# Four early chunks read in one step, two chunks by scan, q and k in two transfers, and a new order of the whole program

## The chip, the cores and the metric

The kernel runs on one core of one Trainium2 chip. The metric is the device time of one execution in microseconds (us). An execution under the profiler gives a trace; other executions give times alone.

## What is computed

Three things in a row: a gated recurrence over time (mLSTM) for 4 batches and 8 heads of 768 steps with head size 40, and then two pairs of dense layers on its output, which is laid out as 3072 tokens of 320 values.

```python
for t in range(S):
    m_new = np.maximum(f_gate[:, :, t] + m, i_gate[:, :, t])
    f_stab = np.exp(f_gate[:, :, t] + m - m_new)
    i_stab = np.exp(i_gate[:, :, t] - m_new)
    C = f_stab * C + i_stab * outer(vt, kt)
    n = f_stab * n + i_stab * kt
    y[:, :, t] = sigmoid(o_gate) * (C @ qt) / np.maximum(np.abs(n @ qt), 1.0)
x = y as (3072, 320)
h = x @ w_in                       # 320 -> 2048
g = np.where(h >= 1, h, np.where(h <= -1, 0.0, (h + 1) ** 2 / 4))
x = g @ w_out                      # 2048 -> 320
h = x @ w2_in
r = np.maximum(h, 0.0)
out = (r * r) @ w2_out
```

## The kernel before

**The recurrence by chunks.** Time is cut into six chunks of 128 steps per batch, 24 chunks in all, ordered chunk 0 of the four batches, then chunk 1 of the four, and so on. Each chunk is two halves of 64 steps. `attention(n, ...)` plans the steps of one chunk. TensorE makes the scores of queries and keys and the products of keys and values for the state (`scores`), VectorE weighs the scores by decay factors (`weigh0`, `weigh1`) and updates the state (`Ca`, `Cb`), and TensorE then reads: the part inside a half (`intra`: weighed scores times values) plus the part from the state (`inter`: query times state).

**Two ways to read.** For the first four chunks (`WIDE = 4`) the read is two steps. `cross` makes the products that go from one half of the partitions to the other, `after` copies a small piece out of them (tile `tiny`), and `read` waits for that copy and makes the rest (`read` and `cross` are recorded on line 904). For the other twenty chunks the read is one step, `wide`: near products (line 904) into the output tile and far products (line 962) into the free part of the score tiles, taken in turn so that all four 64x64 quarters of TensorE's array have work. What landed in the score tiles is then moved (`move1`, `move0`, into tile `yx`) and added (`join1`, `join0`, line 977) by ScalarE and VectorE.

**Two ways to make the decay factors.** For chunks 0 and 1 (`c <= SUMC`), eight chunks in all, they come from `rise` (a product of a mask and the log factors, line 739), `sums` (TensorE, lines 745, 748 and 752: running sums of logs) and an exponential on ScalarE. For the others the raw factors are loaded from a DRAM copy (`ld_f`, tensor `f_all`) and run through a scan on VectorE (`decay`, line 774); the values are then scaled by the input gate first (`v_in`, line 799).

**The dense layers.** The first pair of layers runs in 8 blocks of 3 chunks, the second in 6 blocks of 4 chunks; each block goes over 16 slices of the hidden size. Per block and slice there are 8 products into tile `h` (line 1131), an activation on ScalarE, VectorE and GpSimd, and 3 products per chunk into tiles `acc0`, `acc1`, `acc2` and `v` (line 1191). Numbers are split into a high and a low part, so each product is made more than once. The weights are stored as 64-bit floats and are taken apart on chip when they first come (lines 499 to 551).

**What sets the order.** Nothing runs in the order in which it is written. Each step is put into a `Plan` with its engine, a rank, a duration as the author takes it, and what it needs. `Plan.order()` walks through time with these durations and takes, on each engine, the ready step of the lowest rank; where a step may go to several engines it takes the one that would end first. The result is one fixed order per engine. The ranks come from tables of numbers (`MOVE`, `SHIFT_OF`, `FINE`), the choice of engine also from `PICK`. `LAT["SP"]` is the time from the end of a transfer's issue to its data. Where the plan has nothing for TensorE, it puts one of `FILL = 140` idle steps, two small products each (line 1274), so 280 in all, that keep TensorE active.

**Start.** SyncE (SP) issues all transfers from one queue. The gates come in two parts (lines 574 and 582). A chain of scans and products on VectorE, GpSimd and ScalarE makes logs and factors from them, which TensorE transposes (lines 620 and 661); only then can the first `rise` and `sums` run.

**From one part to the next.** From the tenth chunk on, the output of a chunk goes to DRAM by four transfers (`scatter`, line 433) and comes back transposed by three (`gather`, lines 436 and 438), all issued by SP, before its block can start. The output of a first dense block goes the same way to the second part.

Of the kernel before, what the change touches and what calls it, by code (L numbers as in the profile page):

```python
# [39 lines left out]
class Plan:  # L40
# [7 lines left out]
    LAT = {"T": 0.25, "SP": 1.9}  # L48
# [134 lines left out]
def pool(n):  # L183
# [28 lines left out]
}  # L212
SHIFT_OF = {
    "g": {"v1": 110.65, "v1f": -135.75, "v1i": -162.53, "masks": 80.77, "ft": -115.13, "fc": 118.96,
        "a3": -39.22, "tp": -127.3, "cp": -87.45, "a2": -58.39, "p1": 4.03, "a1": -74.68, "p2": -6.2,
        "v2": -223.95, "d1": -233.43, "d2": 196.83},
    "w": {"load": 53.07, "a_move": 94.67, "v_clamp": -3.04, "a_tail": 53.39, "v_top": -13.26,
        "v_join": 70.33, "a_hi": 176.02, "v_lo": 73.74, "lo": 162.56, "sub": -82.64, "put": 44.29,
        "clamp": 68.16, "top": -29.18},
    "x": {"ld_qk": 35.32, "ld_vko": 9.45, "rise": -96.86, "sums": -140.56, "grow": -39.2, "sumsa": -33.31,  # L220
        "growa": 2.76, "k_in": 53.09, "sig": 9.42, "sigma": -42.83, "q_in": 16.55, "scores": -12.57,
        "update": -52.52, "scale": 48.33, "weigh0": -85.03, "weigh1": 19.6, "cross": -50.09, "after": 5.03,
        "read": -20.72, "norm_a": -53.03, "norm_b": 97.64, "norm_c": 36.58, "tr": 3.8, "hi": 22.16,
        "lo": -67.91, "ld_f": 46.74, "ld_a": -16.53, "decay": 84.93, "v_in": -41.91, "wide": -47.73,
        "move1": -71.31, "join1": -42.21, "move0": 16.41, "join0": -65.28, "turn": 80.21, "store": -67.91,
        "load": -12.79, "again": -79.17, "rise1": -46.24, "sums1": 3.17},
    "y": {"load": 227.79, "hi": 109.08, "lo": 229.83},
    "d": {"mm1": 8.22, "relu": 72.6, "square": 34.95, "gate": -54.05, "hi": 16.25, "lo": 54.66, "mm2": 11.36,
        "keep": -54.24, "evac": -38.36, "turn": -51.89, "store": 169.37},
}  # L230
FINE = {
    "g0": {"v1": -57.95, "v1f": -31.12, "v1i": 73.83, "masks": 45.91, "ft": 91.47, "fc": 26.6, "a3": -16.28,
        "tp": -50.47, "cp": -121.18},
    "g1": {"v1": 97.2, "v1f": 61.71, "v1i": -10.95, "a2": -29.43, "p1": 77.88, "a3": -55.68, "a1": -102.99,
        "p2": -199.57, "v2": 37.26, "d1": -99.65, "d2": -161.28, "tp": 115.56, "cp": 250.13, "ft": -12.8,
        "fc": 74.2},
    "w0": {"load": -48.87, "a_move": -182.32, "v_clamp": 70.39, "a_tail": -9.72, "v_top": 22.93,
        "v_join": -60.58, "a_hi": -60.75, "v_lo": -70.85, "lo": 33.59, "clamp": 7.25, "top": 98.67},
    "w1": {"load": -23.77, "a_move": -21.6, "v_clamp": -53.77, "a_tail": -209.41, "v_top": -57.83,
        "v_join": -140.2, "a_hi": -147.14, "v_lo": -50.52, "lo": -201.67, "clamp": 96.23, "top": -86.1},  # L240
    "w2": {"load": 10.02, "a_move": -103.33, "v_clamp": -20.23, "a_tail": 103.18, "v_top": 18.06,
        "v_join": -156.63, "a_hi": 35.17, "sub": -158.96, "put": -66.82, "clamp": 10.62, "top": 12.98},
    "w3": {"load": 42.08, "a_move": 28.86, "v_clamp": 48.51, "a_tail": 42.67, "v_top": -19.28,
        "v_join": -49.33, "a_hi": 192.52, "sub": 27.7, "put": 13.53, "clamp": 14.13, "top": 39.95},
    "w4": {"load": 20.87, "a_move": 23.82, "v_clamp": 40.5, "a_tail": -13.26, "v_top": 33.13,
        "v_join": 119.88, "a_hi": 70.78, "sub": 81.87, "put": -64.08, "clamp": -55.62, "top": -54.18},
    "w5": {"load": -21.16, "a_move": -42.33, "v_clamp": -72.31, "a_tail": 133.19, "v_top": 74.43,
        "v_join": 126.61, "a_hi": 139.07, "sub": -41.56, "put": -106.72, "clamp": 4.0, "top": 58.13},
    "w6": {"load": 35.35, "a_move": 10.88, "v_clamp": -43.5, "a_tail": 100.1, "v_top": -34.69,
        "v_join": -1.42, "a_hi": 104.74, "sub": -20.29, "put": -136.89, "clamp": -79.27, "top": 6.17},  # L250
    "w7": {"load": 86.26, "a_move": 120.67, "v_clamp": -119.39, "a_tail": -66.48, "v_top": -68.52,
# [1148 lines left out]
```

## Time and profile before

| | |
|---|---|
| runs without profiler, 3 | median 827.92 us (827.0 to 828.84) |
| profiled execution | 832.61 us, span in the trace 830.9 us |
| mean granted TensorE clock | 0.994 of full |
| busy: TensorE products | 819.8 us, 99% |
| busy: VectorE (DVE) | 387.1 us, 47% |
| busy: ScalarE (ACT) | 459.0 us, 55% |
| busy: GpSimd (POOL) | 365.8 us, 44% |

The span is what lies between the first and the last recorded instruction; the profiled execution took 1.7 us more than its span, and 4.7 us more than the median of the runs without a profiler. A busy TensorE is not a TensorE at its peak: products are pipelined, so the recorded duration of one contains time in which others run; how long a step takes is read from the starts of what stands before and behind it.

### The profile page before, as it was taken

The page shows a single profiled execution, that of the slowest core. Times are in us where ns is not written, and L with a number is a line of the kernel's source. Part 1 is how long each engine was busy: PE and PEld are TensorE (multiplying, and loading weights), DVE is VectorE, ACT ScalarE, POOL GpSimd, SP SyncE. Part 2 cuts the span into 40 slices and gives each one's busy share as a digit, 9 for nine tenths or more (in the row PEclk, how much of TensorE's full clock was granted, in tenths as well). Part 3 has the DMA queues.
Part 4 walks back from the last instruction along what each step waited for, and adds up shares of the span by engine and source line. Part 5 has one row for each costly group of instructions (what it writes and reads, how often), then busy time and mean ns, then how long its engine had stood idle before and what let it go on. Part 6 is the DMA issues. An engine that isn't in the chain of part 4 may idle for free.

```text
span 830.9 us, 18844 instructions
## 1 busy us (share of the span) xinstructions
PE 819.8 (99%) x7536; PEld 753.4 (91%) x7536; DVE 387.1 (47%) x760; ACT 459.0 (55%) x897; POOL 365.8 (44%) x387
## 2 busy tenths in 40 slices
PE   8999999999899999999999999999999999999998
PEld 7668899999899999999999988999899898998997
DVE  5678879785676555544225655312121111111111
ACT  4667678866456556555678867443433433433432
POOL 3133220042353467682677566534533534433333
PEclk9899999999999999999999999999999999999999
DMA  8467564435443464521313541002110100100000
GB/s 229 162 220 237 166 172 151 141 108 124 109 116 92 110 150 125 160 56 31 70 41 99 164 98 67 1 0 70 29 42 1 45 26 1 52 1 0 32 1 33
DMA packets 93244, 73.41 MB, mean 88 GB/s; under 512 B 58944, under 2 KB 77372, under 8 KB 93156
## 3 DMA queue, kind: packets, MB, share of 16 engines
q1 hardware_dynamic: 93156, 72.21, 30.5%
q8 instruction: 59, 0.97, 0.5%
q14 instruction: 29, 0.24, 0.1%
HBM read 61.67 MB, written 10.51 MB: 87 GB/s over the span
## 4 chain that ended last, share of the span: by engine, by line
PE 91%; DMA 4%; SPq 1%; DVE 1%; ACT 1%; POOL 1%; issue 0%; POOLq 0%; DVEq 0%
PE h L1131 42%; PE acc L1191 34%; PE v L1191 5%; PE v L904 2%; PE s L850 2%; PE acc L1274 1%; PE s L857 1%; PE h L745 1%; DMA qk<-in_qk_dram 1%; DMA w<-in_gates_dram 1%; DMA vko<-in_vko_dram 1%; PE acc L550 1%; PE h L748 1%; SPq L433 1%; DMA x<-xn 1%
## 5 line engine op out<-in xcount | busy, mean ns | idle before, releaser
L1163 POOL TENSOR_TENSOR xTh<-xTl,xTh 128x512 fp32r<-128x512 f32 x96 | 124.1, 1292 | 177.1 <-ACT xTh L485 176.8
L1191 PE MATMUL acc<-w,g 128*128 128x320 f32 x1152 | 194.9, 312 | 0.1
L1151 DVE TENSOR_TENSOR xTl<-xTl,h 128x512 f32<-128x512 f32 x96 | 66.0, 688 | 245.3 <-ACT xTl L1138 245.3
L1191 PEld LDWEIGHTS acc<-w,g 128*128 128x128 f32 x1152 | 176.0, 188 | 3.3 <-ACT g L485 0.6
L1131 PE MATMUL h<-xTh,w 128*128 128x384 f32 x640 | 176.1, 340 | 2.4 <-ACT xTh L485 2.3
L1191 PE MATMUL acc<-w,xTh 128*128 128x320 f32 x864 | 142.5, 308 | 0.0
L1191 PEld LDWEIGHTS acc<-w,xTh 128*128 128x128 f32 x864 | 134.2, 188 | 8.2
L1131 PE MATMUL h<-qk,w 128*128 128x512 f32 x384 | 135.9, 395 | 0.0
L1131 PE MATMUL h<-xTl,w 128*128 128x384 f32 x384 | 129.9, 338 | 0.6 <-POOL xTl L1092 0.6
L1138 ACT ACTIVATE xTl<-h 128x512 f32<-128x512 f32 x96 | 57.4, 598 | 115.2 <-PE h L1131 112.1
L1131 PEld LDWEIGHTS h<-xTh,w 128*128 128x128 f32 x640 | 117.3, 188 | 3.8 <-ACT xTh L485 2.6
L1136 ACT ACTIVATE r<-h,half 128x384 f32<-128x384 f32 x128 | 74.0, 578 | 79.6 <-PE h L1131 68.2
L1149 DVE SCALAR_TENSOR_TENSOR r<-r,h 128x384 f32<-128x384 f32 x128 | 70.0, 547 | 78.8 <-ACT r L1142 73.5
L485 ACT ACTIVATE xTh<-xTl 128x512 fp32r<-128x512 f32 x96 | 60.7, 632 | 81.9 <-PE v L1191 80.1
L1131 PEld LDWEIGHTS h<-qk,w 128*128 128x128 f32 x384 | 72.1, 188 | 12.9
L1163 POOL TENSOR_TENSOR g<-r,g 128x384 fp32r<-128x384 f32 x63 | 66.3, 1053 | 36.0 <-ACT g L485 35.2
L485 ACT ACTIVATE g<-r 128x384 fp32r<-128x384 f32 x128 | 66.4, 520 | 21.2 <-PE acc L1191 18.3
L1131 PE MATMUL h<-vko,w 128*128 128x512 f32 x192 | 75.7, 394 | 0.0
L1131 PEld LDWEIGHTS h<-xTl,w 128*128 128x128 f32 x384 | 72.4, 188 | 0.9 <-POOL xTl L1092 0.9
L1142 ACT ACTIVATE r<-r 128x384 f32<-128x384 f32 x128 | 66.9, 523 | 2.9
L1131 PE MATMUL h<-d,w 128*128 128x512 f32 x192 | 60.3, 395 | 0.0
L1191 PE MATMUL v<-w,xTh 128*128 128x320 f32 x288 | 57.8, 309 | 0.0
(148 smaller groups left out, 1098.4 us busy)
## 6 DMA issues: line engine op xcount, KB each, us to landing
wraw<-in_wts_dram SPq DMA_DIRECT2D x32, 704.0 KB
vko<-in_vko_dram SPq DMA_DIRECT2D x24, 524.5 KB
d<-f_all SPq DMA_DIRECT2D x32, 128.0 KB
qk<-in_qk_dram SPq DMA_DIRECT2D x24, 160.0 KB
out_dram<-o SPq DMA_DIRECT2D x20, 160.0 KB
qk<-in_qk_dram SPq DMA_DIRECT2D x24, 128.0 KB
x<-x SPq DMA_DIRECT2D x24, 128.0 KB
ab<-a_all SPq DMA_DIRECT2D x20, 128.0 KB
```

The source lines that it names most:

```text
L433: nc.sync.dma_start(out=to[a], in_=t[32 * a:32 * a + 32].rearrange("r (b t) -> r b t", t=32))
L485: nc.scalar.activation(out=out, in_=in_, func=ACTF.Copy)
L850: nc.tensor.matmul(out=z["s"][a][u, U * h:U * h + U], lhsT=z["qk"][row[a], 0, h, u], rhs=z["qk"][row[a], 1, h, u], start=True, stop=True)
L904: nc.tensor.matmul(out=z["y"][sub[u], E * h:E * h + E], lhsT=lhsT, rhs=rhs, start=start, stop=True, skip_group_check=True)
L1131: nc.tensor.matmul(out=h, lhsT=a, rhs=b, start=(i == 0), stop=(i == 7))
L1136: nc.scalar.activation(out=r, in_=z["h"], func=ACTF.Relu, scale=0.5, bias=half)
L1138: nc.scalar.activation(out=r, in_=z["h"], func=ACTF.Relu)
L1142: nc.scalar.activation(out=z["r"], in_=z["r"], func=ACTF.Square)
L1149: nc.vector.scalar_tensor_tensor(out=r, in0=r, scalar=1.0, in1=z["h"], op0=ALU.min, op1=ALU.max)
L1151: nc.vector.tensor_mul(out=r, in0=r, in1=z["h"])
L1163: engine[e].tensor_sub(out=z["g1"], in0=z["r"], in1=z["g0"].bitcast(F32))
L1191: nc.tensor.matmul(out=acc[k][:, 0:DM], lhsT=a, rhs=b, start=(f == f0 and i == 0), stop=(f == f1 - 1 and i == 2))
```

## The change

- `WIDE` goes from 4 to 0: the first four chunks read by `wide` too. In chunk 0 the first half has no state yet, so its step has 24 products where a later chunk has 32; `move1` and `join1` follow, `move0` and `join0` do not.
- `SUMB = 2`: of the four chunks with `c == 1` only those of batches 0 and 1 make their factors by sums; batches 2 and 3 take `ld_f`, `decay` and `v_in`.
- `ld_qk` issues two transfers where it issued three: the first, of 64 rows, now brings k and q.
- The tile of `ft` is kept under a key of its own for each of the two gate parts.
- The planner's durations of transfers are other numbers, `LAT["SP"]` goes from 1.9 to 2.8, and all of `MOVE`, `SHIFT_OF`, `FINE` and `PICK` are new, so every engine's order is new.

```diff
-    LAT = {"T": 0.25, "SP": 1.9}
+    LAT = {"T": 0.25, "SP": 2.8}
...
 MOVE = {
-    "g": [-174.08, -251.94],
+    "g": [-393.49, -318.28],
...
-WIDE = 4
+WIDE = 0
 SUMC = 1
+SUMB = 2
...
-            t_["ft"] = t = new("s", [128, 512])
+            t_["ft", c0] = t = new("s", [128, 512])
...
-            plan.add(Y, rank + GDMA, 0.2, d1, [key["f0"] + e + (1,)], [("f0d", 0)])
+            plan.add(Y, rank + GDMA, 0.33, d1, [key["f0"] + e + (1,)], [("f0d", 0)])
...
+        summed = c < SUMC or c == SUMC and b < SUMB
...
-            for a, w, p in ((0, D, 0), (0, U, 1), (1, D, slice(0, 2))):
-                nc.sync.dma_start(out=z["qk"][U * a:U * a + w, p], in_=qk[n][0:w, p, 4 * a:4 * a + 4])
+            for a, w in ((0, U), (1, D)):
+                nc.sync.dma_start(out=z["qk"][U * a:U * a + w], in_=qk[n][0:w, :, 4 * a:4 * a + 4])
...
-        plan.add(Y, at - 11.5 , 2.1, ld_vko, make=[("vko", n)])
+        plan.add(Y, at - 11.5, 1.3, ld_vko, make=[("vko", n)])
         if c:
-            if c > SUMC:
+            if not summed:
...
-        fx = "h" if early or c == 1 else "s"
+        fx = "h" if early or c else "s"
...
-        if c <= SUMC:
+        if summed:
             plan.add({V: Shared(0.69), P: 1.35, A: 2.05}, at - 7.5 - SUMR * c, 0, rise, [("fmT", c), ("o", -1)], [("d1", n)])
...
-        if c > SUMC:
+        if not summed:
             plan.add(pb(H * E, H), at - 6, 0, v_in, [("vko", n), ("it", c)], [("vt", n)])
...
-            plan.add(Y, at + 0.4, 1.6, store, [("xn", n)], [("xnd", n)])
-            plan.add(Y, at + 0.5, 1.2, load, [("xnd", n)], [("x2", ("n", n))])
+            plan.add(Y, at + 0.4, 1.9, store, [("xn", n)], [("xnd", n)])
+            plan.add(Y, at + 0.5, 1.6, load, [("xnd", n)], [("x2", ("n", n))])
...
-    plan.add(Y, -40, 0.8, cst_rest, make=[("cst", 0)])
+    plan.add(Y, -40, 1.9, cst_rest, make=[("cst", 0)])
```

What the new tables move is seen in the order of the instructions. Three places follow; a row is a line of the program, the operation, and what it writes and reads (a number behind `x` counts equal rows), and "..." stands for rows left out.

**SyncE at the very start**, before:

```order
L709 DMA vko<-in_vko_dram 128x1049
L574 DMA w_178<-in_gates_dram 36x2x128
L576 DMA ident<-in_cst_dram 128x128
L499 DMA wraw<-in_wts_dram 128x1408
L582 DMA w_178<-in_gates_dram 36x2x640
L709 DMA vko<-in_vko_dram 128x1049
L499 DMA wraw<-in_wts_dram 128x1408
L705 DMA qk<-in_qk_dram 40x512
L705 DMA qk<-in_qk_dram 64x512
L705 DMA qk<-in_qk_dram 40x2x512
```

and with the change:

```order
L710 DMA qk<-in_qk_dram 64x2x512
L710 DMA qk<-in_qk_dram 40x2x512
L578 DMA w_173<-in_gates_dram 36x2x128
L580 DMA ident<-in_cst_dram 128x128
L503 DMA wraw<-in_wts_dram 128x1408
L710 DMA qk<-in_qk_dram 64x2x512
L710 DMA qk<-in_qk_dram 40x2x512
L586 DMA w_173<-in_gates_dram 36x2x640
L714 DMA vko<-in_vko_dram 128x1049
L503 DMA wraw<-in_wts_dram 128x1408
```

The second part of the gates (36x2x640) was the fifth transfer, behind one large `vko`; it is now the eighth, behind four transfers of q and k, and the first `vko` stands behind it.

**TensorE at the read of an early chunk**, before (tile `d_935` holds the weighed scores of the fourth chunk; lines 745 and 748 are the sums of another):

```order
L904 MATMUL v<-Ca,qt 64x41 x4
L1069 MATMUL s<-ident,xn 128x128 x3
L745 MATMUL h<-d_577,o 64x512 x2
...
L904 MATMUL v<-vko,d_935 64x41 x8
L904 MATMUL v<-Ca,qt 64x41 x4
L904 MATMUL v<-vko,d_935 64x41 x8
L550 MATMUL acc_165<-wt,ident 128x352
```

and with the change (the first chunk):

```order
L770 MATMUL h<-o,logs 64x64 x8
L909 MATMUL v<-vko,d_525 64x41 x2
L967 MATMUL s<-Ca,qt 64x41
L967 MATMUL s<-vko,d_525 64x41
...
L909 MATMUL v<-vko,d_525 64x41
L909 MATMUL v<-Ca,qt 64x41
```

The four products of `cross` stood apart, ahead of other work; now near and far products are one run, and the far ones go to tile `s`.

**SyncE at the store and reload of the twelfth chunk** (`xn_133`; `x_18`, `x_1` and `x_7` are outputs of the first dense part), before:

```order
L721 DMA ab<-a_all 40x512
L715 DMA d_3369<-f_all 64x512 x2
L433 DMA x_18_107<-pa 32x10x32 x4
L433 DMA x_1_90<-pa 32x10x32 x4
L433 DMA x_7_96<-pa 32x10x32 x4
L433 DMA xn_133<-xn 32x10x32 x4
L709 DMA vko<-in_vko_dram 128x1049
L436 DMA x_3567<-xn_133 128x2x128
L438 DMA x_3567<-xn_133 64x128 x2
```

and with the change:

```order
L437 DMA xn_133<-xn 32x10x32 x4
L714 DMA vko<-in_vko_dram 128x1049
L720 DMA d_3437<-f_all 64x512 x2
L714 DMA vko<-in_vko_dram 128x1049
L440 DMA x_3515<-xn_133 128x2x128
L442 DMA x_3515<-xn_133 64x128 x2
L437 DMA x_18_107<-pa 32x10x32 x4
L437 DMA x_1_90<-pa 32x10x32 x4
L437 DMA x_7_96<-pa 32x10x32 x4
```

The twelve transfers of the dense outputs stood ahead of the chunk's store; they now stand behind its reload.

Counted over the whole order: the idle products are 280 in both; 230 of them stood ahead of the first `sums`, now 246 do. Between the twelfth chunk's scores and the first product of the block that takes it in stood 6 groups of eight products of line 1131 and 78 products of line 1191; now there are 16 groups and 144 products. The runs of equal array form (64x64 quarters or the whole array) change 108 times before and 102 times with the change.

## Rows read from the trace of the kernel before

**Rows 1.** The page, part 1: busy time, share, instructions.

```profile
PE 819.8 (99%) x7536; PEld 753.4 (91%) x7536; DVE 387.1 (47%) x760; ACT 459.0 (55%) x897; POOL 365.8 (44%) x387
```

**Rows 2.** Waits of TensorE: who waited for whom, us in total, times, longest.

```profile
PE h L1131 <- ACT xTh L485: 2.3, 1, 2.3
PE s L620 <- POOL w L599: 1.9, 1, 1.9
...
PE v L904 <- DVE sg L1025: 0.7, 1, 0.7
```

**Rows 3.** Stretches: length; busy PE, PEld, DVE, ACT, POOL; granted clock, DMA share, GB/s.

```profile
20.00:25.00 5.00, 5.00 (x40) 5.00 (x39) 4.09 (x7) 2.86 (x4) 0.00 (x0) 0.50 0.67 214
...
50.00:150.00 100.00, 99.79 (x1288) 86.48 (x1287) 84.46 (x188) 75.64 (x159) 25.09 (x35) 1.00 0.55 174
...
200.00:250.00 50.00, 47.06 (x620) 44.57 (x619) 33.45 (x76) 25.75 (x55) 22.66 (x25) 0.97 0.43 109
```

**Rows 4.** Timeline of TensorE, 1 to 26 us: start, us, instruction.

```profile
1.26 12.78 PE L1274 MATMUL acc<-x 128*128 128x160 bf16 x160 [1.26 <-DVE w L578]
...
19.34 6.47 PE L1274 MATMUL acc<-x 128*128 128x160 bf16 x52
25.74 0.65 PE L745 MATMUL h<-d,o 64*64 64x512 f32 x2
```

**Rows 5.** Timeline of all engines, 0 to 45 us.

```profile
3.27 0.81 SPq L582 DMA_DIRECT2D w<-in_gates_dram  x1
...
5.22 2.10 SPq L705 DMA_DIRECT2D qk<-in_qk_dram  x3
...
10.34 1.54 DVE L592 TENSOR_TENSOR_SCAN w<-w,w 36x640 f32<-36x640 f32 x1 [0.69 <-DMA w<-in_gates_dram]
```

**Rows 6.** Timeline of TensorE, 40 to 110 us: reads, sums, a wide read.

```profile
43.17 0.25 PE L904 MATMUL acc<-Ca,qt 40*64 40x41 f32 x1
...
43.76 0.86 PE L550 MATMUL acc<-wt,ident 128*128 128x352 f32 x2
...
44.70 0.66 PE L904 MATMUL acc<-vko,d 64*64 64x41 f32 x16
...
45.90 0.27 PE L765 MATMUL h<-o,logs 64*64 64x64 f32 x1
...
60.53 1.08 PE L745 MATMUL h<-d,o 64*64 64x512 f32 x4
...
62.51 0.61 PE L904 MATMUL v<-vko,d 64*64 64x41 f32 x16
...
63.99 0.86 PE L550 MATMUL acc<-wt,ident 128*128 128x352 f32 x2
...
69.24 0.26 PE L904 MATMUL v<-vko,d 64*64 64x41 f32 x2
...
70.31 0.44 PE L1131 MATMUL h<-xTh,w 128*128 128x384 f32 x1
```

**Rows 7.** Timeline of SyncE's queue, 196 to 232 us.

```profile
211.27 5.86 SPq L433 DMA_DIRECT2D x<-pa  x12
```

**Rows 8.** The chain that ended last, 205 to 235 us: start, us, what.

```profile
206.13 1.52 PE acc L1191 x9
207.65 1.43 PE h L1131 x8
...
223.11 4.55 DMA x<-xn
...
229.42 2.32 PE h L1131 x7
```

**Rows 9.** Groups by line: busy us, mean ns of one, idle before.

```profile
L1274 PE MATMUL acc<-x 128*128 128x160 bf16 x280 | 25.8, 259 | 1.3 <-DVE w L578 1.3
```

**Rows 10.** Groups by line and form, VectorE: busy us, mean ns, idle before.

```profile
L774 DVE TENSOR_TENSOR_SCAN d<-d,eyes 128x512 f32<-128x512 f32 x16 | 20.2, 1264 | 13.1 <-PE s L962 13.0
...
L977 DVE TENSOR_TENSOR v<-s,yx 64x164 f32<-64x164 f32 x40 | 13.5, 338 | 2.0 <-ACT yx L485 0.7
```

More of the change, by code (lines that the diff above doesn't have):

```diff
@@ L220 @@
[L220 to L226, printed above, removed]
@@ L230 @@
+    "y": {"load": 181.09, "hi": 187.73, "lo": 276.44},
+    "d": {"mm1": 15.93, "relu": 96.16, "square": 31.54, "gate": -58.92, "hi": 128.93, "lo": 51.88,
+        "mm2": 18.41, "keep": -69.51, "evac": -57.39, "turn": -17.6, "store": 185.58},
 }
 FINE = {
[L232 to L236, printed above, removed]
@@ new lines @@
+    "w14": {"load": -57.58, "a_move": -39.21, "a_tail": 125.41, "v_top": -4.28, "clamp": 157.03,
+        "top": -4.65, "v_join": -38.99, "a_hi": 142.25, "v_lo": -36.37, "lo": -96.21},
+    "x0": {"ld_qk": -24.49, "ld_vko": 37.5, "rise": 22.48, "sums": -236.91, "grow": 23.29, "sumsa": -11.81,
+        "growa": -11.63, "k_in": 8.17, "sig": -143.29, "sigma": -82.1, "q_in": -162.17, "scores": -152.9,
+        "update": -97.61, "scale": -264.07, "weigh0": -168.27, "weigh1": 76.56, "cross": -21.08,
+        "after": -242.75, "read": -6.93, "norm_a": 37.85, "norm_b": -148.44, "norm_c": 63.94, "tr": 4.79,
+        "hi": 33.77, "lo": -247.23, "again": -25.03, "wide": -26.58, "move1": -98.78, "join1": -47.55},
@@ new lines @@
+    "x1": {"ld_qk": -49.09, "ld_vko": 8.73, "rise": -66.25, "sums": -21.24, "grow": -51.63, "sumsa": -3.58,
+        "growa": -54.77, "k_in": -145.19, "sig": -119.92, "sigma": -78.23, "q_in": -117.64, "scores": -187.4,
+        "update": 15.39, "scale": -33.91, "weigh0": -2.86, "weigh1": 352.02, "cross": -32.47, "after": 76.29,
+        "read": -38.74, "norm_a": -129.96, "norm_b": -60.93, "norm_c": -45.07, "tr": -62.29, "hi": -5.23,
+        "lo": -147.46, "again": 215.21, "wide": -101.25, "move1": -131.17, "join1": -156.55},
@@ new lines @@
+    "x2": {"ld_qk": -43.67, "ld_vko": -46.08, "rise": -0.12, "sums": 32.79, "grow": -95.11, "sumsa": 62.82,
+        "growa": -92.13, "k_in": -18.36, "sig": -148.62, "sigma": -190.57, "q_in": -182.77,
+        "scores": -152.84, "update": -15.28, "scale": -14.61, "weigh0": 122.39, "weigh1": 105.42,
+        "cross": -9.47, "after": 94.1, "read": -53.54, "norm_a": 3.86, "norm_b": -52.47, "norm_c": -61.37,
+        "tr": -25.92, "hi": -34.21, "lo": 110.55, "again": 57.68, "wide": -63.84, "move1": -135.82,
+        "join1": -208.24},
@@ new lines @@
+    "x3": {"ld_qk": 29.97, "ld_vko": -19.9, "rise": 53.45, "sums": 164.04, "grow": -49.09, "sumsa": 76.41,
+        "growa": -23.21, "k_in": 6.41, "sig": -53.99, "sigma": 139.4, "q_in": -25.85, "scores": -31.75,
+        "update": 32.8, "scale": -1.75, "weigh0": 208.34, "weigh1": 4.06, "cross": -129.77, "after": 128.44,
+        "read": -184.85, "norm_a": 6.35, "norm_b": -7.46, "norm_c": 6.3, "tr": 22.85, "hi": -51.43,
+        "lo": -147.34, "again": -202.46, "wide": -105.24, "move1": -71.28, "join1": -254.77},
@@ L1244, in dense @@
                 ok = ("pa", (part, n), 99)
-            plan.add(Y, g + 2, 0.7 if part else 1.6, store, [ok], [("st", (part, n))])
+            plan.add(Y, g + 2, 0.7 if part else 1.9, store, [ok], [("st", (part, n))])
     def x2_load(n, at):
```

237 lines of the change are left out of this document (113 added, 124 removed), and 32 rows, old and new, of tables (FINE, MOVE).

## The prediction, made before the changed kernel ran

> **What bounds the kernel now.** I read the busy shares first. TensorE is busy 99% of the span [rows 1], so what it has to do, plus the little time it waits, is the time. Busy here counts the 280 idle products as well [rows 9]. So the question for every part of the change is one of two: does it take work out of TensorE's line, or does it move a wait?
>
> The waits of TensorE come next. After the start there is one large one, near 228 us, on data that came back from DRAM: the first product of a block waited 2.3 us for the ScalarE copy of it [rows 2]. The stretch around it has the granted clock at 0.97 and only 47.06 of 50 us busy, so 2.9 us were lost there in all [rows 3], and the chain through it shows why it was late: twelve transfers of dense outputs held SyncE's queue for 5.86 us from 211.27 on [rows 7], the chunk's own store and reload stood behind them, and the reload landed 4.55 us after 223.11 [rows 8].
>
> Then the start. 160 idle products took 12.78 us, 0.080 us each; the 52 that stand right ahead of the first `sums` took 25.74 - 19.34 = 6.40 us, 0.123 each [rows 4], because the granted clock was at 0.50 there, the level of 1.2 GHz, after TensorE had waited 1.9 us for GpSimd [rows 2, 3]. The `sums` themselves could not start earlier than those idle products ended: the order of an engine is fixed.
>
> Last, the engines beside it. From 50 to 150 us VectorE is busy 84.46 of 100 us [rows 3]. That is the one place where another engine could take over.
>
> **The change, part by part.** The sum is made against the profiled execution, 832.6 us. That one is 4.7 us above the median of the unprofiled runs, 827.92 us; I carry the difference over to the median unchanged.
>
> *Two chunks by scan.* Two `sums` leave TensorE. One takes from 60.53 to 62.51, 1.98 us, where nothing stands between [rows 6], and in that stretch TensorE is never without work [rows 3]. 2 x 1.98 = **-4.0 us**. In exchange VectorE gets two scans of 1.26 us [rows 10], and SyncE four more transfers of factors. Both lie beside TensorE's work; if VectorE's cover goes, see the third rival.
>
> *Four chunks by one read.* Before: `cross` of the second chunk from 43.17 to 43.76, 0.59 us; its `read` from 44.70 to 45.90, 1.20 us; the fourth chunk's `read` from 62.51 to 63.99, 1.48 us [rows 6]. One wide read takes from 69.24 to 70.31, 1.07 us, with 32 products [rows 6]. The new ones have 24, but the fullest quarters still make eight, so I take 1.07 whole. The gain per chunk is then at least 1.48 - 1.07 = 0.4 us, if `cross` lies hidden among other products, and at most 0.59 + 1.48 - 1.07 = 1.0 us. I take 0.7: 4 x 0.7 = **-2.8 us**, between -1.6 and -4.0. What it adds off TensorE is one `move1` and one `join1` per chunk, 0.34 us on VectorE for the join [rows 10], and the copy into `tiny` goes.
>
> In the trace, the twenty chunks that read this way already made TensorE wait for VectorE only 0.7 us, once [rows 2]. The Trainium skill, "TensorEngine Tiling (Array Packing)", section "PSUM Bottleneck", speaks against this part: "Tiling speeds up TensorE but not PSUM evacuation", so that the copies out can become the limit. By that rule the four joins would stand on the path, 4 x 0.34 = 1.4 us of the 2.8 would be lost, and the whole sum would end 1.4 us higher; the waits here bear it out only for that single 0.7 us.
>
> *The order at the start.* The idle products are 280 in both, and 246 instead of 230 stand ahead of the first `sums`. So 16 fewer stand behind it: 16 x 0.080 = **-1.3 us** [rows 4]. When the first `sums` start has two sides. Right ahead of it are 44 idle products instead of 52: at the full clock 44 x 0.080 = 3.5 us, at the half 5.4, against 6.40. That is a gain of 2.9 or 1.0 us. Against it, the second part of the gates is issued later. Before, it was issued at 3.27 and its scan began at 10.34 [rows 5], so it was landing, not issuing, that took the time. Now four transfers of q and k stand ahead of it. They cost 2.10 / 3 = 0.70 us of issue each [rows 5], 2.8 us in all, less the large transfer that moved behind. So the gate chain is between 0 and 2.8 us later; I take 1.0, since most of the seven microseconds was waiting for data. Together that is between -2.9 and +1.8, and I take **-1.0 us**.
>
> *q and k in two transfers.* Each chunk's issue is one transfer shorter, 0.70 us of SyncE [rows 5], 24 times. SyncE is not on the path except where a store stands behind it. I cost it at nothing; what covers it is that loads are issued long ahead. If that cover is gone, it counts in my favour.
>
> *The wait near 228 us.* In the new order the twelfth chunk's store and reload stand ahead of the twelve transfers instead of behind them. And there is more between: before, 6 groups of eight first-layer products and 78 second-layer products stood between that chunk's scores and the block that needs it, 6 x 1.43 + 78 / 9 x 1.52 = 21.8 us [rows 8]; now 16 groups and 144 products, 47 us. So I take this wait as gone: 2.9 us [rows 3], and the slow clock behind it. Seven products took 2.32 us there, where eight take 1.43 a moment earlier [rows 8]: 2.32 - 7 x 0.179 = 1.1 us. Together **-4.0 us**, between 0 and -4.4 with the scores that follow.
>
> *New waits.* A new order of every engine has waits of its own that no row of the old one can show. At best none; at worst what the old order had, some 8 us with its clock. I take one of the size of the largest now, **+2.9 us** [rows 3].
>
> The sum: -4.0 - 2.8 - 1.3 - 1.0 - 4.0 + 2.9 = -10.2. The profiled execution would take 822.4 us, the median of the runs 817.7.
>
> **The rivals.**
>
> *Only the work goes.* The start gains nothing, because what was an idle product is now a plain wait, and the wait near 228 us turns up at another reload. For it: the idle products only stood where the plan saw nothing to do, and taking 16 of them out of the chain does not bring forward what it waits for. Against it: the 47 us of cover. Then -4.0 - 2.8 = -6.8, 821.1 us.
>
> *Everything goes and no new wait comes.* -13.1, 814.8 us. For it: from 50 to 200 us the old order had almost no wait either. Against it: every rank is new.
>
> *VectorE becomes the bound, and the kernel is slower.* Between 50 and 150 us it is busy 84.46 us [rows 3]. The change adds two scans and up to four joins, 2 x 1.26 + 4 x 0.34 = 3.9 us, and TensorE's own work there shrinks by the 6.8 us of the first two parts. VectorE would have to do 88.4 us of work in 93.2 us, 95%. If its waits for others keep it at today's 84.5%, that stretch takes 88.4 / 0.845 = 104.6 us, 4.6 longer than now; the gain of the first two parts is gone, and the reload comes late again with its VectorE steps. With the 2.3 us won at the start: 827.9 + 4.6 - 2.3 = 830.2 us. It decides as soon as VectorE cannot go above some 90% there. Against it: it already fits 84% with 0.2 us of TensorE waiting, and part of its work was early, when it had time.
>
> **How the numbers follow.** The forecast as summed gets 0.60, only the work 0.20, no new wait 0.13, VectorE 0.07. The time is the first one's, 817.7. The range goes from 812 (the best bounds: -4.0 - 4.0 - 1.3 - 2.9 - 4.4 = -16.6 gives 811.3) to 825, which takes in the second rival and another wait of 3.9 us on top of it. The third rival and an accumulation of bounds are left out. A measurement of this kernel can tell about 0.2% from no change, 1.7 us. Of the cases only the third rival is slower; the second can come close to no change if two more waits of that size appear. So faster 0.88, same 0.05, slower 0.07.
>
> **What would show it.** In the profile after: six `sums` instead of eight, and 18 VectorE scans of factors instead of 16; an early wide read of about 1.07 us; the first `sums` at 23 to 25.7 us; no wait of TensorE on a reload in the stretch from 200 to 250 us; VectorE at 88 to 92% between 50 and 150 us. It would be wrong if TensorE waits more than 3 us in total between 30 and 800 us, if the first `sums` starts after 27 us, or if a wide read of a first chunk takes as long as the two old steps.

## The result, and the profile after

The changed kernel took 838.98 us in the median of 4 executions (835.2 to 840.26), the kernel before 827.46 us beside it. The ratio is 1.0135, with a 95% interval from 1.0093 to 1.0176: slower by 11.5 us, where 10.2 us less were forecast. Seven more executions later (changed_again, below) gave 837.25 us and 1.0088 (1.0058 to 1.0118). So it is slower by about 1%, and the second number counts as much as the first. Here and below a ratio leaves out executions over 1.5% above the fastest of the same kernel (847.65 us in changed_again, 847.39 in weights_first), which the medians hold.

| | before | after |
|---|---|---|
| median of the runs | 827.46 us | 838.98 us |
| profiled execution | 832.61 us | 835.2 us |
| its span | 830.9 us | 833.4 us |
| its mean granted clock | 0.994 | 0.992 |
| span less busy time of TensorE | 11.1 us | 20.5 us |

The two profiled executions are only 2.6 us apart. The time of either kernel goes with TensorE's granted clock: of 31 executions of the kernel before, those at 1.000 took 824.4 to 827.5 us and those at 0.994 took 831.5 to 832.9, and its profiled one was such a 0.994; the first four of the changed kernel had 0.988 to 0.992. So the profile before is that of a long execution.

The page, part 1, of the changed kernel, as in [rows 1], and its waits of TensorE, as in [rows 2]:

```profile
PE 812.9 (98%) x7516; PEld 750.5 (90%) x7516; DVE 402.7 (48%) x766; ACT 450.0 (54%) x896; POOL 368.1 (44%) x387
```

```profile
PE acc L554 <- ACT w L489: 5.1, 2, 4.0
PE s L624 <- POOL w L603: 3.8, 1, 3.8
PE s L855 <- issue: 2.4, 2, 1.7
...
PE s L1074 <- DVE v L982: 1.2, 1, 1.2
```

TensorE is busy 6.9 us less, near the 6.8 that the first two parts promise, and has 9.4 us more of idle time. The stretches tell where. After (columns as in [rows 3]):

```profile
20.00:25.00 5.00, 5.00 (x38) 4.61 (x38) 4.19 (x8) 3.73 (x9) 0.00 (x0) 0.50 0.56 151
20.00:40.00 20.00, 20.00 (x239) 14.15 (x240) 12.90 (x23) 10.79 (x19) 1.74 (x2) 0.86 0.31 94
30.00:40.00 10.00, 10.00 (x155) 6.03 (x155) 6.07 (x11) 4.86 (x8) 1.74 (x2) 1.00 0.01 2
40.00:60.00 20.00, 17.48 (x356) 11.43 (x355) 14.50 (x41) 9.08 (x18) 4.49 (x8) 1.00 0.91 249
50.00:150.00 100.00, 89.40 (x1318) 78.47 (x1315) 80.14 (x183) 68.07 (x150) 31.86 (x40) 0.97 0.66 182
60.00:80.00 20.00, 13.97 (x213) 11.12 (x214) 11.52 (x27) 12.14 (x25) 9.62 (x12) 0.83 0.67 200
200.00:250.00 50.00, 49.95 (x482) 48.69 (x481) 36.85 (x78) 32.51 (x67) 19.75 (x24) 1.00 0.62 149
```

and four of the same stretches before:

```profile
20.00:40.00 20.00, 20.00 (x241) 13.74 (x239) 13.15 (x24) 11.99 (x20) 2.46 (x3) 0.88 0.47 163
30.00:40.00 10.00, 10.00 (x159) 6.12 (x155) 7.39 (x14) 6.15 (x12) 1.72 (x2) 1.00 0.28 90
40.00:60.00 20.00, 19.95 (x414) 14.40 (x410) 14.24 (x39) 13.02 (x28) 5.72 (x10) 1.00 0.71 224
60.00:80.00 20.00, 19.94 (x312) 15.37 (x312) 16.50 (x41) 15.83 (x33) 7.29 (x12) 1.00 0.74 245
```

From 40 to 80 us TensorE idles 2.5 + 6.0 = 8.5 us where it idled 0.1, and the clock is at 0.83 in the second half. The wait near 228 us is gone: 49.95 of 50 us busy instead of 47.06, at the full clock. And the DMA column shows something that no wait of TensorE names: from 30 to 40 us the DMA engines stood still (0.01, 2 GB/s), and then they were busy 0.91 of the time.

SyncE's queue says why. Its timeline after:

```profile
0.81 1.64 SPq L710 DMA_DIRECT2D qk<-in_qk_dram  x2
...
4.36 1.42 SPq L710 DMA_DIRECT2D qk<-in_qk_dram  x2
5.82 0.80 SPq L586 DMA_DIRECT2D w<-in_gates_dram  x1
...
26.49 0.33 SPq L503 DMA_DIRECT2D wraw<-in_wts_dram  x1
38.66 1.43 SPq L710 DMA_DIRECT2D qk<-in_qk_dram  x2
40.20 0.41 SPq L503 DMA_DIRECT2D wraw<-in_wts_dram  x1
...
52.41 0.42 SPq L503 DMA_DIRECT2D wraw<-in_wts_dram  x1
```

and the one row before that has no match there:

```profile
23.24 8.85 SPq L499 DMA_DIRECT2D wraw<-in_wts_dram  x3
```

Two places. First, four transfers of q and k go ahead of the second part of the gates, which is issued at 5.82 instead of 3.27 [rows 5]. Second, the load of q and k for the third chunk is next behind the weights of 26.49. There are two buffers for q and k; it waits for the scores of the first chunk, which run at 38 us, and all that stands behind it in the one queue waits too. Before, three loads of weights went out between 23.24 and 32.09, ahead of that load; now the next goes at 40.20. TensorE's and VectorE's rows show what follows from the first place [rows 4, 5]:

```profile
13.60 1.54 DVE L596 TENSOR_TENSOR_SCAN w<-w,w 36x640 f32<-36x640 f32 x1 [6.82 <-DMA w<-in_gates_dram]
```

```profile
19.24 0.43 PE L624 MATMUL s<-ident,w 36*128 36x36 f32 x2 [3.81 <-POOL w L603]
...
24.33 3.79 PE L1279 MATMUL acc<-x 128*128 128x160 bf16 x44
28.05 1.08 PE L750 MATMUL h<-d,o 64*64 64x512 f32 x4
```

The scan starts 3.26 us later, TensorE waits 3.81 us instead of 1.95, and the first `sums` start at 28.05 instead of 25.74. From the second place, the chain that ended last, near 60 us:

```profile
40.20 6.75 DMA wraw<-in_wts_dram
...
52.41 9.88 DMA wraw<-in_wts_dram
62.31 0.84 ACT wraw L515
63.15 0.37 ACT xTh L489
63.52 0.36 ACT w L489
63.92 1.54 PE acc L554 x2
```

That load of 704 KB takes 9.88 us from issue to landing, with the DMA engines at 0.97 from 50 to 60 us; ScalarE, whose order is fixed, waits for it and so makes the copy that TensorE needs late, and TensorE waits 3.99 us. The first product of the dense layers starts at 74.94 us, 66.85 before.

### The profile page after: what moved, and what is told of

It reads as the page before. It is cut to its first block, busy times and chain, and to the rows that moved or that the text cites. A ratio compares the mean times of both kernels' runs of the same rounds, so it can differ in the third digit from the quotient of the medians.

```text
span 833.4 us, 18747 instructions
## 1 busy us (share of the span) xinstructions
PE 812.9 (98%) x7516; PEld 750.5 (90%) x7516; DVE 402.7 (48%) x766; ACT 450.0 (54%) x896; POOL 368.1 (44%) x387
## 4 chain that ended last, share of the span: by engine, by line
PE 88%; DMA 5%; DVE 3%; SPq 2%; ACT 1%; issue 1%; POOL 0%; DVEq 0%; ACTq 0%
PE h L1136 41%; PE acc L1196 34%; PE v L1196 5%; DMA wraw<-in_wts_dram 3%; PE v L909 2%; DMA qk<-in_qk_dram 2%; PE s L855 2%; PE acc L1279 1%; PE s L862 1%; PE acc L554 1%; SPq L437 1%; DVE wt L519 1%; SPq L710 0%; PE s L967 0%; PE h L750 0%
## 5 line engine op out<-in xcount | busy, mean ns | idle before, releaser
L1196 PEld LDWEIGHTS acc<-w,xTh 128*128 128x128 f32 x864 | 131.4, 188 | 0.7
L1168 POOL TENSOR_TENSOR g<-r,g 128x384 fp32r<-128x384 f32 x61 | 64.4, 1058 | 55.2 <-ACT g L489 46.5
## 6 DMA issues: line engine op xcount, KB each, us to landing
vko<-in_vko_dram SPq DMA_DIRECT2D x24, 524.5 KB
```

Of the source, the lines that this page charges most:

```text
L1168: engine[e].tensor_sub(out=z["g1"], in0=z["r"], in1=z["g0"].bitcast(F32))
L1196: nc.tensor.matmul(out=acc[k][:, 0:DM], lhsT=a, rhs=b, start=(f == f0 and i == 0), stop=(f == f1 - 1 and i == 2))
```

## The experiments

The theory after this reading: the time is lost in SyncE's queue at the start, in two places, and reaches TensorE by the gate chain and by the weights. The rivals: the new steps themselves make the waits (the one read, the scans), or the new form of the q and k transfers does.

In most of them single steps are moved in the finished order and nothing is planned anew. Behind the loop of `Plan.order()` stands then:

```diff
-        return [(self.steps[i][2], on[i]) for _, i in out]
+        seq = [i for _, i in out]
+        at = lambda k: next(j for j, i in enumerate(seq) if (self.tags[i], self.steps[i][2].__name__) == k)
+        for a, b in BEHIND:
+            i = seq.pop(at(a))
+            seq.insert(at(b) + 1, i)
+        return [(self.steps[i][2], on[i]) for i in seq]
```

`AHEAD` does the same with `seq.insert(at(b), i)`. A step is named by its chunk or slice and its function. The ratios are against the kernel before on the same chip, whose median there was 827.2 to 829.2 us.

| run | executions | median us | ratio (95%) |
|---|---|---|---|
| gates_first | 10 | 836.49 | 1.0089 (1.0054 to 1.0124) |
| weights_first | 10 | 834.65 | 1.0068 (1.0042 to 1.0094) |
| gates_and_weights | 10 | 835.86 | 1.0082 (1.0049 to 1.0116) |
| third_buffer | 10 | 836.25 | 1.0091 (1.0060 to 1.0123) |
| qk_behind_values | 10 | 832.15 | 1.0059 (1.0036 to 1.0081) |
| qk_behind_and_weights | 10 | 831.61 | 1.0039 (1.0013 to 1.0064) |
| fixed_gates_ahead | 12 | 830.04 | 1.0025 (1.0005 to 1.0045) |
| weights_ahead | 6 | 833.23 | 1.0074 (1.0049 to 1.0100) |
| weights_ahead_buffer | 6 | 836.05 | 1.0113 (1.0075 to 1.0151) |
| two_reads_new_order | 6 | 834.97 | 1.0082 (1.0049 to 1.0115) |
| two_reads_fixed | 8 | 834.31 | 1.0075 (1.0050 to 1.0101) |
| changed_again | 7 | 837.25 | 1.0088 (1.0058 to 1.0118) |
| before_two_transfers | 10 | 829.77 | 1.0013 (0.9986 to 1.0040) |
| before_qk_first | 7 | 831.80 | 1.0058 (1.0031 to 1.0084) |
| before_gates_ahead | 12 | 826.92 | 0.9998 (0.9972 to 1.0025) |
| sums_only | 10 | 831.62 | 1.0018 (0.9986 to 1.0049) |
| wide_only | 4 | 845.16 | 1.0173 (1.0138 to 1.0208) |
| parts_old_order | 4 | 846.38 | 1.0201 (1.0173 to 1.0229) |

**The two places by themselves.**

```diff
+BEHIND = [((("x", 0), "ld_qk"), (None, "gate_rest")), ((("x", 1), "ld_qk"), (("x", 0), "ld_qk"))]
```

> The changed kernel, with the two loads of q and k that stood ahead of the second part of the gates put right behind it on SyncE; nothing else is moved. Theory (the start of SyncE's queue costs the time): the second gate part is issued near 3.3 us instead of 5.82, its scan starts near 10.3 instead of 13.60, TensorE waits about 3 us less before 20 us and the first sums start near 25 us instead of 28.05; the time falls by 2 to 4 us, to some 835 to 837 against a before of 827.5, a ratio near 1.010. Rival (the four transfers only stood in front of a wait for other data, so the new work or another place costs the time): scan after 12.5 us or first sums after 27 us, the time unchanged within 1 us, ratio 1.0135.

```diff
+BEHIND = [((("x", 2), "ld_qk"), (("w", 3), "load"))]
```

> The changed kernel, with the load of q and k for the third chunk, which held SyncE's queue from 26.8 to 38.66 us, put behind the next load of weights. Theory (that load blocks the queue, so weights land late, ScalarE stands in order behind them and TensorE behind ScalarE): the load of weights is issued near 35 us instead of 40.20, as soon as its buffer is free, TensorE's idle time between 40 and 80 us falls from 8.6 to 3 to 6 us, and the time by 3 to 7 us, a ratio of 1.005 to 1.010. Rival (weights are late for their buffers, not for the queue; the waits between 40 and 80 us come from the new work on VectorE and ScalarE): idle time between 40 and 80 us stays above 7.5 us, the ratio at 1.0135, or higher by the third chunk's own lateness.

> The changed kernel with both edits: the second gate part ahead of the loads of q and k, and one load of weights ahead of the third chunk's. Theory: the two gains add, first sums near 25 us, idle time of TensorE between 40 and 80 us at 3 to 6 us, 829 to 834 us, a ratio of 1.002 to 1.008. Rival (new work, or the order further on, costs the time): above 1.012.

Both lie below the changed kernel's 1.0135, but neither is clear of its second measurement, 1.0088, and gates_and_weights, with both lists, does not add them up. So the times show no gain of these three; what they do is seen in the traces. Rows of gates_first, of SyncE, ScalarE and TensorE, show what it missed:

```profile
2.85 0.81 SPq L592 DMA_DIRECT2D w<-in_gates_dram  x1
```

```profile
14.42 0.47 ACT L827 ACTIVATE sg<-vko 128x320 f32<-128x320 f32 x1 [5.40 <-DMA vko<-in_vko_dram]
```

```profile
22.23 0.50 PE L671 MATMUL s<-ident,w 36*128 36x36 f32 x5 [3.82 <-ACT logs L634]
```

The scan now starts at 8.71, but ScalarE stands in order before a `vko` that comes behind q and k, and makes its copy of the logs late. The first `sums` start at 27.45, on the rival's side. In weights_first the next load of weights is the second of this pair and is out by 32.21, 8 us earlier than 40.20:

```profile
25.52 6.69 SPq L509 DMA_DIRECT2D wraw<-in_wts_dram  x2
```

TensorE's wait on ScalarE comes at 52.34 and is 1.75 us long, and TensorE idles 4.5 us between 40 and 80 us instead of 8.5, as my theory had it.

One trace is not enough for the start. Five traces share the changed kernel's first loads up to the gates (the changed kernel's two, weights_first, third_buffer, two_reads_new_order): their scans start from 12.62 to 14.90 and their first `sums` from 25.86 to 29.50. In five with the old first loads (the kernel before, before_two_transfers, wide_only, sums_only, parts_old_order) it is 9.23 to 10.34 and 21.58 to 25.74. So the later scan is no accident of one execution; a difference of 2 us between two single traces may be one.

**The form of the transfers.** The edit is the one of `ld_qk` in the diff of the change, alone.

> The kernel before, its own order, with q and k in two transfers instead of three and nothing else. Theory (the form of the transfer is worth nothing by itself): ratio 1.000 within 0.002, SyncE's q and k issues 1.4 us long instead of 1.7 to 2.1, waits of TensorE as before. Rival (the wider transfer lands later and is the cause of the loss): ratio 1.005 or more, with TensorE or VectorE waiting for q and k.

No difference that can be told, and in the trace 1.48 and 1.62 us for the first two pairs of transfers: the form is not the cause.

**q and k behind all that the gate chain stands behind.** `cst_rest`, a constant, goes with them.

```diff
+BEHIND = [((("x", 0), "ld_qk"), (("x", 1), "ld_vko")), ((("x", 1), "ld_qk"), (("x", 0), "ld_qk")), ((None, "cst_rest"), (("x", 1), "ld_qk"))]
```

> The changed kernel with the first two chunks' q and k put behind both vko loads and one load of weights, and not only behind the gates as in gates_first; nothing else is moved. There ScalarE had waited 5.4 us for one vko and stood behind the other and a load of weights (landing at 17.8 and 20.9 us) before it could copy the logs, so TensorE still waited 3.8 us. Theory (these loads stand in order before the gate chain on ScalarE too): the vko and weights land 3 to 4 us earlier, TensorE waits under 1.5 us in all between 14 and 25 us, first sums near 24 to 26 us instead of 27.45, ratio 1.003 to 1.007. Rival (the start is worth no more than gates_first showed): ratio 1.009.

With `((("x", 2), "ld_qk"), (("w", 3), "load"))` in the list besides:

> The changed kernel with both: the first two q and k behind vko and weights, and the third chunk's q and k behind the next load of weights. Theory: the waits at the start and the half clock behind them go, those near 52 to 60 us shrink to under 2 us: ratio 1.000 to 1.004, the clock at 0.996 or more in most runs. What stays is the order behind 60 us. Rival (the waits only move to another wait further on, as when gates and weights were put first together): ratio 1.006 to 1.010.

The start is mended: first `sums` at 24.28 in the one and 23.76 in the other, earlier than in any trace with the changed kernel's first loads, and between 20 and 40 us the clock is at 1.00 where it was 0.86. Rows of qk_behind_values:

```profile
20.00:40.00 20.00, 17.68 (x330) 11.59 (x329) 11.83 (x23) 10.06 (x18) 1.73 (x2) 1.00 0.43 144
40.00:60.00 20.00, 15.24 (x290) 9.88 (x285) 12.90 (x37) 10.34 (x20) 7.87 (x11) 1.00 0.89 267
```

The second row is what stays: TensorE idles 4.8 us there, with the DMA engines at 0.89. By time, 1.0059 is clear of the changed kernel's 1.0135 and not of 1.0088; 1.0039 (up to 1.0064) just touches the interval of the second (from 1.0058).

**The same fault put into the kernel before.**

```diff
+AHEAD = [((("x", 0), "ld_qk"), (None, "gate_rest")), ((("x", 1), "ld_qk"), (None, "gate_rest"))]
```

> The kernel before, with the six transfers of q and k of its first two chunks put ahead of the second part of the gates; nothing else is moved. Theory (that is what delays the start): the gates' issue moves from 3.27 to about 7.5 us, the scan from 10.34 to 13.5 us or later, first sums 2 to 4 us later, half clock in the stretch behind in more of the runs, ratio 1.004 to 1.009. Rival (the scan waits for something else, or the time at the start is made up later): ratio 1.000 to 1.002.

As the theory has it. The gates' issue, the scan, TensorE's wait and the stretch behind it:

```profile
7.12 0.82 SPq L592 DMA_DIRECT2D w<-in_gates_dram  x1
```

```profile
14.41 1.54 DVE L602 TENSOR_TENSOR_SCAN w<-w,w 36x640 f32<-36x640 f32 x1 [4.52 <-DMA w<-in_gates_dram]
```

```profile
20.04 0.43 PE L630 MATMUL s<-ident,w 36*128 36x36 f32 x2 [5.18 <-POOL w L609]
```

```profile
20.00:40.00 20.00, 19.96 (x199) 13.36 (x203) 13.78 (x23) 11.40 (x21) 1.73 (x2) 0.83 0.48 162
```

One move of loads (here six transfers of q and k) costs an otherwise untouched kernel 4.8 us (0.0058 of 827.47). So such a start is shown to cost time. How much of the changed kernel's loss it is, is less sure, as the overlap of 1.0059 and 1.0088 says.

**A buffer instead of an order.**

The planner goes on reckoning with two, so that the order stays.

```diff
+    bufs["qk"] = 3
     pools = {}
...
-    plan = Plan(bufs)
+    plan = Plan({**bufs, "qk": 2})
```

> The changed kernel, its own order, with a third buffer for q and k, so that the third chunk's load has nothing to wait for. Theory (that load's wait for a buffer held the queue): the load issues near 27 us instead of 38.66, the next weights near 35 us, and the time falls as with the weights put first, to a ratio of 1.003 to 1.010. Rival (the queue's block hid nothing, the weights wait for their own buffers): idle time of TensorE between 40 and 80 us within 1 us of the changed kernel's 8.6, ratio 1.012 or above.

The load went out at 28.19 and the weights at 34.81, as expected, and TensorE's idle time between 40 and 80 us fell from 8.5 to 6.6 us. The ratio, 1.0091, lies in my range, but it is no lower than the changed kernel's second measurement, so no gain of time is shown:

```profile
28.19 1.44 SPq L711 DMA_DIRECT2D qk<-in_qk_dram  x2
34.81 0.34 SPq L504 DMA_DIRECT2D wraw<-in_wts_dram  x1
42.12 0.33 SPq L715 DMA_DIRECT2D vko<-in_vko_dram  x1
```

The next load in the queue, a `vko`, has two buffers as well and waits until 42.12. The block moved one place on.

**The parts without their order.** wide_only and sums_only are the kernel before with one part each, parts_old_order has all three; the planner makes the order again from the old tables. The one read takes the ranks of `cross` and `read`, moves and joins rank first, and in sums_only and parts_old_order `v_in` of two chunks is ranked earlier.

```diff
...
-WIDE = 4
+LIKE = {"wide": "cross", "move1": "read", "join1": "read"}
+WIDE = 0
...
```

> All three parts of the change (one read for the first four chunks, two chunks by scan, two transfers of q and k) with the tables, durations and so nearly the order of the kernel before; the new steps take the ranks of the steps they replace. Theory (the parts gain 6.8 us on TensorE, the new order costs more than that): SyncE's start as before, TensorE's idle time between 40 and 100 us under 2 us, 820 to 825 us, a ratio of 0.991 to 0.997. Rival (the parts themselves make the waits, by their steps on VectorE and ScalarE or their transfers): ratio above 1.008 with TensorE waiting 6 us or more between 40 and 150 us.

> The kernel before, with one read for the first four chunks and nothing else; the new steps take the ranks of cross and read. Theory (a read in one step saves 0.4 to 1.0 us a chunk): ratio 0.995 to 0.998, an early wide read from 1.07 to 1.3 us. Rival (moves and joins on VectorE stand on the path of the early chunks): ratio above 1.002, TensorE waiting for a join or a move.

> The kernel before, with two chunks more by scan and nothing else. Theory (two sums of 1.98 us leave TensorE): ratio 0.994 to 0.997, six sums. Rival (the factors of these two chunks come later by the way over DRAM and the scan): ratio 1.000 or above, TensorE waiting near 60 to 110 us for scores or weighing of the seventh or eighth chunk.

Here my theory was wrong. The rivals' figures came: 1.0201 with 15.0 us of idle time between 40 and 150 us in parts_old_order, 1.0173 in wide_only, 1.0018 in sums_only. Their reasons came in part only. The read itself took what was forecast (wide_only, TensorE):

```profile
36.53 0.25 PE L908 MATMUL v<-vko,d 64*64 64x41 f32 x2
...
37.59 1.28 PE L1278 MATMUL acc<-x 128*128 128x160 bf16 x16
...
59.46 0.83 PE L854 MATMUL s<-qk 40*64 40x64 f32 x27 [1.34 <-DVE xTl L1096]
...
141.64 0.90 PE L1073 MATMUL s<-ident,xn 128*128 128x128 f32 x3 [4.14 <-DVE xn L1029]
```

1.06 us from 36.53 to 37.59, and the first `sums` start at 21.58. Waits of up to 4.14 us appear, one of them 100 us later and on outputs of a later chunk. In parts_old_order two waits are the rival's own, 0.65 us of scores on a move at 49.26 and 2.37 us of transposes on a join at 107.81. A reason that fits is that the far products lie in the score tiles, of which there are two, and hold them until the join, so that the plan gives scores and transposes, which need these tiles too, other places; it is argued from the plan and not tested. These runs do not price the parts: the order differs as well, and that the old tables do not fit the new steps is as likely a cause as the steps. For the one read the next runs keep the order. For the two chunks by scan there is no such run, and sums_only, 1.0018 (0.9986 to 1.0049), shows no gain of it.

**Two reads in the new order.** At the place of the one read stand `cross`, the copy and `read`; moves and joins do nothing.

```diff
+        if early:
+            def wide():
+                cross()
+                after(A)
+                read()
...
         used = [("qt", n), ("Ca", n)] + ([("Cb", n - 1)] if c else [])
```

> The changed kernel in its own order, in which the first four chunks read again in two steps: at the place of the one read stand cross, the copy by ScalarE and read; moves and joins are left out, so the score tiles are free earlier and VectorE has 4 times 0.67 us less. Theory (order and transfers cost the time, the one read is a small gain): 2 to 5 us slower than the changed kernel, ratio 1.016 to 1.020. Rival (the one read holds the two score tiles until its joins are done, scores and transposes of other chunks wait for them, and that is where the time goes): faster than the changed kernel, ratio 1.010 or less.

> The changed kernel once more, for more executions. Both theories: a ratio of 1.010 to 1.017; mean granted clock 0.986 to 0.993 in most executions, against 0.994 to 1.000 for the kernel before.

> The changed kernel with q and k behind vko and weights, as in qk_behind_and_weights (1.0039), and the first four chunks read in two steps again, at the same places. Theory of the forecast (one read saves 0.4 to 1.0 us a chunk): slower than qk_behind_and_weights by 1.6 to 4 us, a ratio of 1.006 to 1.009. Rival (the one read holds both score tiles until its joins and keeps other work waiting, more than it saves): a ratio of 1.002 or below.

The seven further executions missed my range of 1.010 to 1.017 with 1.0088. Against the first four, two reads (1.0082) looked 4 us faster, as the rival had it; against the further ones they are the same. On the mended start, where less else hides it, two reads have a ratio of 1.0075 and one read 1.0039: 0.0036, or 3.0 us, in the direction and of the size forecast. The intervals still overlap, so the gain is likely, not shown.

**The gates further ahead, and the rest of the loss.** `AHEAD = [((None, "gate_rest"), (("w", 0), "load"))]` in the kernel before, and in qk_behind_and_weights:

> The kernel before with the second part of the gates put ahead of the first load of weights on SyncE, and nothing else. Theory (the scan waits for the gates' landing behind 704 KB of weights, TensorE's wait of 1.95 us follows from it and the half clock from that wait): scan 1 to 3 us earlier than 10.34, TensorE's wait near 16 us gone or under 1 us, clock 0.998 to 1.000 in most executions, ratio 0.996 to 0.999. Rival (the idle products end no earlier, and the weights come later for it): ratio 1.000 or above.

> qk_behind_and_weights with the second part of the gates ahead of the first load of weights too. Theory: TensorE's wait of 2 us ahead of the first sums shrinks, ratio 1.001 to 1.003. Rival (that wait is for the products on VectorE behind the weights' steps, not for the gates; the weights come later): ratio 1.004 or above.

In the kernel before it is worth nothing: the scan starts at 8.80, the wait near 16 us is gone, the first `sums` come at 21.07, and the time is the same: a later start costs time, an earlier one than before gains none. In the changed kernel the first `sums` come at 22.93. What is left then, on TensorE:

```profile
55.18 1.54 PE L564 MATMUL acc<-wt,ident 128*128 128x352 f32 x2 [2.97 <-ACT w L499]
65.18 0.63 PE L865 MATMUL s<-qk 40*64 40x64 f32 x27 [1.72 <-issue]
...
102.22 0.63 PE L865 MATMUL s<-qk 40*64 40x64 f32 x27 [1.65 <-issue]
```

The wait of 2.97 us is again the one for ScalarE behind weights. The last two runs put three more loads of q, k and `vko` behind loads of weights, and the second of them adds the third buffer. The list then ends with:

```diff
+BEHIND = [..., ((("x", 3), "ld_qk"), (("w", 7), "load")), ((("x", 5), "ld_qk"), (("w", 10), "load")), ((("x", 4), "ld_vko"), (("w", 6), "load"))]
```

> fixed_gates_ahead with three more loads of weights ahead of the loads of q, k and vko that stood in front of them waiting for a buffer. Theory (each of these loads goes out 1 to 3.5 us earlier, into a gap of the queue): TensorE's wait of 2.97 us near 55 us falls under 1 us and the half clock behind it goes, ratio 0.996 to 1.001. Rival (the weights' own steps on ScalarE and VectorE set that wait, or q, k and vko come later for it): ratio 1.002 or above, the wait still over 2 us.

> The same with a third buffer for q and k. Theory: loads of q and k no longer hold the queue, waits of TensorE on them (up to 1.7 us at a place between 60 and 110 us) go, ratio 0.994 to 1.000. Rival (those waits are for score tiles that transposes still hold): no difference to weights_ahead beyond 1 us.

Both are slower than fixed_gates_ahead. TensorE in weights_ahead, and the chain there:

```profile
53.11 0.86 PE L564 MATMUL acc<-wt,ident 128*128 128x352 f32 x2 [1.23 <-ACT w L499]
...
62.85 0.33 PE L977 MATMUL s<-vko,d 64*64 64x41 f32 x1 [6.10 <-DVE Cb L896]
```

```profile
51.54 9.61 DMA vko<-in_vko_dram
...
61.28 0.73 POOL kt L826
62.01 0.43 POOL cx L891
...
62.47 0.34 DVE Cb L896
```

The wait on the weights fell from 2.97 to 1.23 us, and the `vko` that was put behind them became the last one: 9.61 us from issue to landing, and a wait of 6.10, which is 5.59 with the third buffer. In fixed_gates_ahead the same `vko`, issued 0.96 us earlier, was in use at 57.38. From 50 to 60 us the DMA engines are at 0.99 in weights_ahead, so there the order of loads only chooses who waits. For the changed kernel one reason is what was brought earlier: between 20 and 40 us the kernel before moves 163 GB/s and the changed one 94, 1.4 MB less, two loads of weights. It is not the whole reason: weights_ahead moves 170 GB/s there, and 202 from 0 to 40 us where the kernel before moves 196, and still waits.

No version of the changed kernel beat the kernel before. The best, fixed_gates_ahead, stays 0.25% above it (1.0005 to 1.0045) with less work on TensorE; it idles 8.2 us between 40 and 150 us. It is also the only one whose interval is clear of both measurements of the changed kernel (changed_again ran on the same chip beside it), so moving loads alone is shown to take away most of the loss; how that divides between the two places is not shown. What keeps the forecast gain from coming stays open: no order without these waits was found.

## Why the prediction was wrong

*What bounds the kernel*: right. TensorE is the bound, and VectorE did not become it: 80.14 of 100 us between 50 and 150, less than the 88 to 92 that I wanted to see, because TensorE was held up by others. The third rival, the only slower one, falls; the slower case came by another mechanism.

*Two chunks by scan and four one-step reads*, -6.8: right as work. Six `sums` are left, 18 scans, and TensorE's busy time fell by 6.9 us. That it meets 6.8 so closely is partly luck: busy time holds the slow stretches of both traces. The 0.59 us that I read for `cross` also held six products of line 765 that run between its own, so my upper bound of 1.0 us a chunk was too high. In the changed kernel the wide read of the third chunk takes 1.05 us, 57.20 to 58.25, behind 0.54 us of waiting for weighed scores. By the rule of the Trainium skill, "TensorEngine Tiling (Array Packing)", section "PSUM Bottleneck", 1.4 us of it would have gone to the joins; the only waits of TensorE on a join are 1.2 us at 108.10 and 0.3 at 328.68, both behind later chunks, so this trace does not bear it out for the first four.

*The wait near 228 us*, -4.0: right in kind and place. 2.9 us of idle time are gone and the clock there is at 1.00. Its size scatters: in three other traces with the old order the block waited 1.0 to 2.2 us for ScalarE's copy, not 2.3.

*q and k in two transfers*, nothing: right for the form (1.0013). Its reason, "SyncE is not on the path except where a store stands behind it", is the first step that failed. SyncE's queue was on the path where a load at its head waited 11.8 us for a buffer, until 38.66.

*The order at the start*, -1.3 and -1.0: wrong in sign; TensorE's idle time there grew by 1.4 us. The gate chain came 3.26 us later, outside the 0 to 2.8 that I gave, and the first `sums` 2.3 us later, past the 27 us that I named as a sign of being wrong. I took only 1.0 of the 2.8 us of issue, since most of the seven microseconds to the scan was waiting for data. But that wait moved along with the issue: from issue to scan it is 7.07 us before, 7.78 after and 7.29 in before_qk_first. What goes ahead also has to be brought, 832 KB of q and k, and behind it come `vko` and weights that ScalarE waits for in its order. With all of it put back, the ratio came down to 1.0059, from 1.0135 and 1.0088 in its two measurements.

*New waits*, +2.9: the term that decided, and mis-sized. From 40 to 150 us TensorE idled 8.5 + 2.9 = 11.4 us against 0.3 before, and between 30 and 800 us I had named 3 us as a sign of being wrong. From 60 to 70 us the clock is at 0.66 with TensorE busy 6.08 us, which by my estimate takes 0.34 x 6.08 = 2.1 us of the busy time besides. Even my bound of 8 was too low, since it was taken from what the old order had. It could have been seen: the order of SyncE showed the third chunk's load ahead of the weights, and two buffers for q and k meant that it had to wait for the first chunk's scores. I looked at three places and not at this one.

The sum against the profiled execution is then: work -6.9; idle time at the start +1.4, from 40 to 80 us +8.4, from 100 to 150 +2.7, near 228 us -2.9, elsewhere -0.3 together: +2.4, where the spans differ by 2.5. The rest of the 11.5 us between the medians is not in these two traces; the clocks listed beside the runs (0.988 to 0.992 against 0.994 to 1.000) go with it, and from 20 to 40 us the clock is at 0.83 in before_qk_first, behind its wait of 5.18 us, and at 1.00 in before_gates_ahead, without one.

## What to carry to other kernels

When an order is new, read the transfer queue first, item by item: which load at its head has to wait for a buffer, until when, and which loads that others wait for stand behind it. Count what the transfers ahead bring, not only how long they take to issue, and look for stretches in which the DMA engines stand still before one in which they are full. Price new waits from the new order's own dependencies; the waits of the old order are no bound for them. And run the kernel that everything is compared with again: four executions said 1.0135, the next ones 1.0088, and some gains rest on which of the two is taken.

## What was not expected of the hardware

A load of 704 KB took 6.75 us to land from 40.20 and 9.88 us from 52.41, with the DMA engines at 0.91 and 249 GB/s between 40 and 60 us; one of 524.5 KB took 9.61 us from 51.54 in weights_ahead. The second part of the gates, issued at 5.82 to 5.84 us in five traces, was scanned from 12.62 to 14.90. TensorE's waits of 3.81 and 3.99 us in the changed kernel were each followed by a granted clock of 0.50, the level of 1.2 GHz, and two products of 63.92 took 1.54 us there, 0.86 in the same kind of row at the full clock [rows 6]; behind the wait of 2.32 us in qk_behind_values the clock stayed at 1.00, though the kernel before had 0.50 behind one of 1.9 [rows 2, 3]. These runs do not tie the clock to the length of a wait alone.
